# Rebuilding the head of a fused attention and feed-forward kernel

## The chip, the cores and the metric

The kernel runs on one core of a Trainium2 chip. The metric is the device time of one execution in microseconds (us). Engines are named as the profile names them: PE is TensorE (matmuls; PEld are its weight loads), DVE is VectorE, ACT is ScalarE, POOL is GpSimd, and SP issues most DMAs. A "q" behind a name (SPq, ACTq) is that engine's queue of issues.

## What is computed

2048 tokens of 512 features are normalised. A linear attention with 32 heads of 16 and a feed-forward layer of 1792 with the Mish activation both read the normalised tokens, and both are added to the input.

```
xn = _layernorm(x, axis=-1)
return x + _A_ref(xn, A_wqkv, A_w_phi, A_wo) + _B_ref(xn, B_w1, B_b1, B_w2)

# _A_ref
pq = einsum("bhsd,hdf->bhsf", q, w_phi);  pk = einsum("bhsd,hdf->bhsf", k, w_phi)
phi_q = concat([softmax(pq), softmax(-pq)], -1);  phi_k = concat([softmax(pk), softmax(-pk)], -1)
kv = einsum("bhsf,bhsd->bhfd", phi_k, v);  z = einsum("bhsf->bhf", phi_k)
o = einsum("bhqf,bhfd->bhqd", phi_q, kv) / (einsum("bhqf,bhf->bhq", phi_q, z)[..., None] + 1e-6)
return o.transpose(...) @ wo
# _B_ref
h = x @ w1 + b1;  return (h * tanh(softplus(h))) @ w2
```

## The kernel before

The tokens are 16 tiles of 128, in four groups of four (`NG`, `TPG`). The order of all instructions is written by hand: each engine runs its own instructions in the order of the program text, and waits where it needs another engine's or a DMA's result.

The head (L368 to L437) loads inputs and weights and brings group 0 up to its first projection. `fold_turn` (L87) transposes the k part of the weights on PE, 4 x 4 blocks, and ACT copies them to `wT`. `fold` (L101) multiplies them by `Wbd`, a block-diagonal form of `w_phi` (eight blocks of 16x16, made by multiplying `w_phi` with a 0/1 block mask, L409), which gives the folded weight `wkp`. The mask is made on PE (L400): `h16`, an 8x128 selection made on POOL, is multiplied by itself into `pm` in PSUM. `KVmask` (L419, L420) is a copy of it.

`ln_stats` (L118) makes mean and variance on DVE and the reciprocal root on POOL; `ln_apply` (L133) makes the normalised tile `xn` on DVE. For group 0 PE transposes `xn` (`ln_turn_pe`, L144); for the other groups a DMA does (`ln_turn_dma`, L152, issued by SP, two tiles at a time), and the result is `xnT`. `logits` (L196) projects a tile with `wkp` and ACT copies the result to `p_sb`; `value` (L168) projects it with `wv` into `vext`; `hidden` (L176) does units of the first feed-forward layer, four matmuls of 512 columns each, and ACT applies Mish with the bias `b1f`. `extremes` (L202, ten DVE operations) subtracts each head's maximum and minimum; `exponentials` (L227) follow on ACT, two instructions.

The loop over stages `s` (L441) does, for each stage: exponentials of group `s`, `accumulate` of the group before, values, the next group's logits, statistics and transposes of the group after next, `normalise`, and some hidden units, 16 in stage 0. The last loop (L469) makes the attention outputs and the second layer.

All PE results of the head and of the loop (`ptrw`, `ptr`, `pfold`, `pproj`, `ph`, `pm`) share one ring of four PSUM buffers (tag "mm", L59), taken in program order: PE can start a result only when the one four places earlier has been copied out by ACT or DVE.

In the head SP issues, in order: tiles 0-1, 2-3 and 4-7 of `x`, `w1_sb`, `wv`, the q part of `wqk`, tiles 8-15, `w2_sb`, `wo`, and then the two DMA transposes of group 1 (L153). ACT issues the k part of `wqk` and `wsrc` (`w_phi`); POOL issues the bias `b1b`, element by element across partitions.

Of the kernel before, what the change touches and what calls it, by code (L numbers as in the profile page):

```python
# [17 lines left out]
def kernel(  # L18
# [30 lines left out]
    b1_v = B_b1.rearrange("(f p) -> p f", p=P)  # L49
# [21 lines left out]
    b1b = wts.tile([P, FT], BF16, name="b1b")  # L71
# [7 lines left out]
    h16 = consts.tile([8, 8, 16], BF16, name="h16")  # L79
# [322 lines left out]
    st1 = ln_stats(2, 2)
    wT = fold_turn(D)

    nc.sync.dma_start(wo_sb, wo_v[:, :, :])
    xn = lnp.tile([P, TPG, D], BF16, name="xn", tag="xn")
    ln_apply(0, 2, *st0, xn, 0)
# [27 lines left out]
    normal(TPG, st, xn)  # L435
    extremes(0)
# [4 lines left out]
    for s in range(5):  # L441
        exponentials(s)
        if s > 0:
            accumulate(s - 1)
        if s < NG:
            for i in range(2):
                value(s * TPG + i, dve)
        for i in range(TPG):
            logits(s + 1, i, act)
        if s < NG:  # L450
            for i in range(2, TPG):
                value(s * TPG + i, act)
# [12 lines left out]
        hidden((16, 14, 6, 10, 4)[s])
        extremes(s + 1)
# [55 lines left out]
```

## Time and profile before

| | us |
|---|---|
| median of 3 runs (206.18 to 208.66) | 208.13 |
| the profiled execution | 208.03 |
| its span, first to last instruction | 206.30 |
| PE busy | 180.4 (87%) |
| DVE busy | 166.1 (81%) |
| ACT busy | 112.4 (54%) |
| POOL busy | 8.6 (4%) |

The busy shares are averages over stages with different limits: DVE is busy nearly throughout the middle of the kernel, PE throughout its last third, and neither in the head. What a change in the head is worth is read from the waits there: who waits last for whom, until one engine works on without a pause. All times below are microseconds from the span's start. In a timeline row, the bracket at the end is the engine's idle time before the row and what released it.

### The profile page before, as it was taken

Reading aid. Unit: us, or ns where it says so; the run is one execution under the profiler, and the core shown is the slowest. Engines: PE = TensorE matmul, PEld = TensorE weight load, DVE = VectorE, ACT = ScalarE, POOL = GpSimd, SP = SyncE. Lnnn points to the kernel's source line nnn. Section 1 sums busy time; section 2 is a strip of 40 time slices with the busy share of each in tenths; the row PEclk is TensorE's granted clock in tenths of the full one; section 3 lists DMA queues with packets and bytes.
Section 4 is the critical chain, followed back from the end, with each engine's and each line's share of the span. In section 5 each row is a group of like instructions: output and inputs, shape, how many; then the busy total and the mean of one; then the engine's idle time right before and its main releaser. Section 6 shows DMA issues by size and latency. Waiting matters only on the chain.

```text
span 206.3 us, 2689 instructions
## 1 busy us (share of the span) xinstructions
PE 180.4 (87%) x1026; PEld 91.8 (44%) x1041; DVE 166.1 (81%) x270; ACT 112.4 (54%) x141; POOL 8.6 (4%) x22
## 2 busy tenths in 40 slices
PE   0399729999999999899998787599999999999993
PEld 0374303445544464464454243244554455445541
DVE  2857999991599989998999999988879998954502
ACT  2348774887988789999988945131603152000000
POOL 5302001000020000000000000000000000000000
PEclk9999966999999999999999999579999999999998
DMA  5999993100005000000000560763156515567041
GB/s 147 263 385 348 348 143 65 38 0 0 3 2 102 0 3 0 0 3 0 0 0 4 97 106 2 146 126 84 54 102 130 125 51 105 104 152 101 4 102 51
DMA packets 41132, 18.02 MB, mean 87 GB/s; under 512 B 32672, under 2 KB 40608, under 8 KB 41120
## 3 DMA queue, kind: packets, MB, share of 16 engines
q1 hardware_dynamic: 40016, 17.31, 36.6%
q10 hardware_dynamic: 1056, 0.54, 1.1%
q8 instruction: 8, 0.13, 0.3%
q0 software_dynamic: 48, 0.00, 0.1%
q14 instruction: 4, 0.03, 0.1%
HBM read 7.88 MB, written 2.10 MB: 48 GB/s over the span
## 4 chain that ended last, share of the span: by engine, by line
PE 47%; DVE 36%; DMA 9%; ACT 3%; issue 2%; POOL 1%; SPq 0%
PE po L349 20%; DVE s L234 9%; PE pproj L162 8%; PE po L357 7%; PE ph L182 7%; DVE m L211 5%; DMA xnT<-xn 5%; DVE e L244 4%; DVE e L220 4%; DVE stats L124 3%; PE pnd L328 3%; ACT e L230 3%; DVE r L269 3%; DMA x_sb<-in_A_x_dram 3%; DMA ob<-ob 2%
## 5 line engine op out<-in xcount | busy, mean ns | idle before, releaser
L182 PE MATMUL ph<-xnT,w_sb 128*128 128x512 bf16 x224 | 49.3, 379 | 1.8 <-ACT p_sb L200 1.8
L349 PE MATMUL po<-w_sb,acts 128*128 128x512 bf16 x218 | 49.3, 379 | 0.3
L230 ACT ACTIVATE e<-e 128x2048 bf16<-128x2048 bf16 x16 | 29.7, 1902 | 21.9 <-DVE e L220 21.9
L189 ACT ACTIVATE acts<-ph,b1f 128x512 bf16<-128x512 f32 x56 | 36.3, 688 | 4.7 <-PE ph L182 4.6
L234 DVE TENSOR_REDUCE s<-e 128x128 f32<-128x2048 bf16 x16 | 36.4, 2276 | 1.1 <-ACT e L230 1.1
L182 PEld LDWEIGHTS <-w_sb 128*128 128x128 bf16 x224 | 21.9, 98 | 28.3 <-issue 2.1
L349 PEld LDWEIGHTS <-acts 128*128 128x128 bf16 x224 | 21.7, 98 | 25.5
L162 PEld LDWEIGHTS <-xnT 128*128 128x128 bf16 x192 | 19.3, 102 | 29.8 <-DMA xnT<-xn 5.6
L200 ACT CAST p_sb<-pproj 128x512 bf16<-128x512 f32 x32 | 17.5, 587 | 22.7 <-PE pproj L162 21.3
L162 PE MATMUL pproj<-wkp,xnT 128*128 128x512 bf16 x62 | 16.4, 417 | 5.4 <-DMA xnT<-xn 5.2
L357 PE MATMUL po<-wqk,ob 128*128 128x512 bf16 x62 | 16.4, 411 | 2.8 <-DMA ob<-ob 2.8
L364 DVE TENSOR_TENSOR x_sb<-po,x_sb 128x512 bf16<-128x512 f32 x16 | 10.6, 686 | 8.6 <-PE po L357 8.6
L162 PE MATMUL pproj<-wqk,xnT 128*128 128x512 bf16 x62 | 15.1, 392 | 0.3 <-issue 0.2
L162 PE MATMUL pproj<-wv,xnT 128*128 128x512 bf16 x61 | 15.0, 379 | 0.2
L124 DVE BATCH_NORM_STATS2 stats<-x_sb 128x6 f32<-128x512 bf16 x16 | 10.0, 680 | 3.3 <-DMA x_sb<-in_A_x_dram 3.3
L211 DVE TENSOR_TENSOR m<-m 128x512 bf16<-128x512 bf16 (+1 forms) x32 | 11.5, 358 | 1.1
L211 DVE TENSOR_TENSOR m<-p_sb 128x1024 bf16<-128x1024 bf16 x16 | 11.0, 684 | 1.1 <-ACT p_sb L200 1.1
L337 DVE TENSOR_TENSOR ob<-pnd,rd 128x512 bf16<-128x512 f32 x16 | 11.1, 692 | 0.6
L170 DVE CAST vext<-pproj 128x512 bf16<-128x512 f32 x8 | 5.4, 689 | 7.4 <-PE pproj L162 7.2
L357 PEld LDWEIGHTS <-ob 128*128 128x128 bf16 x64 | 6.4, 103 | 10.5 <-DMA ob<-ob 3.0
L336 DVE RECIPROCAL rd<-pnd 128x32 f32<-128x32 f32 x16 | 5.6, 350 | 6.6 <-PE pnd L328 6.6
L328 PE MATMUL pnd<-kvm,qT 128*128 128x136 bf16 x128 | 9.1, 223 | 2.1 <-DMA qT<-e 1.3
(52 smaller groups left out, 149.1 us busy)
## 6 DMA issues: line engine op xcount, KB each, us to landing
w_sb<-in_B_w_dram SPq DMA_DIRECT2D x2, 1792.0 KB, 14.3
out_dram<-x_sb SPq DMA_DIRECT2D x16, 128.0 KB, 1.8
x_sb<-in_A_x_dram SPq DMA_DIRECT2D x1, 1024.0 KB, 14.4
wqk<-in_A_wqkv_dram ACTq DMA_DIRECT2D x1, 512.0 KB, 5.2
x_sb<-in_A_x_dram SPq DMA_DIRECT2D x2, 256.0 KB, 4.8
x_sb<-in_A_x_dram SPq DMA_DIRECT2D x1, 512.0 KB, 8.0
wv<-in_A_wqkv_dram SPq DMA_DIRECT2D x1, 512.0 KB, 13.0
wqk<-in_A_wqkv_dram SPq DMA_DIRECT2D x1, 512.0 KB, 13.4
```

What stands on the lines that cost most here:

```text
L124: nc.vector.bn_stats(stats[:, i, :], x_sb[:, t0 + i, :])
L162: nc.tensor.matmul(pp[:], lhsT=xnT[:, t, kt, :], rhs=w[:, kt, :], start=(kt == 0), stop=(kt == KT - 1),)
L182: nc.tensor.matmul(ph[:], lhsT=w1_sb[:, kt, f * P : (f + 1) * P], rhs=xnT[:, g * TPG : (g + 1) * TPG, kt, :], start=(kt == 0), stop=(kt == ...
L189: nc.scalar.activation(acts[:, f, g * 512 : (g + 1) * 512], ph[:], ACT.Mish, bias=b1f[:, f : f + 1])
L200: copy(p_of[s][:, i, :], pp[:])
L211: nc.vector.tensor_tensor(out=m[:], in0=src[:, :, 0:half], in1=src[:, :, half : 2 * half], op=op)
L230: nc.scalar.activation(v, v, ACT.Exp)
L234: nc.vector.reduce_sum(t[:], e_of[s][:, :, 2 * k : 2 * k + 2, :].rearrange("p l t (c e) -> p l (t c) e", e=16), axis=AX.X,)
L328: nc.tensor.matmul(pnd[:, j, 0:136], lhsT=qT[:, pl * 8 + i * 4 + j, :], rhs=kvm[:, 2 * j + pl, :], start=(pl == 0), stop=(pl == 1),)
L337: nc.vector.tensor_tensor(out=o_t[:, i, :].rearrange("p (j h d) -> p j h d", j=4, d=16), in0=pnd[:, :, 0:128].rearrange("p j (h d) -> p j ...
L349: nc.tensor.matmul(po[:], lhsT=acts[:, f, t * P : (t + 1) * P], rhs=w2_sb[:, f, :], start=(f == 0), stop=False,)
L357: nc.tensor.matmul(po[:], lhsT=oT[:, i * 4 + j, :], rhs=wo_sb[:, j, :], start=False, stop=(j == 3),)
```

## The change

The block mask is made on POOL over 128 partitions (`block`, two selections) instead of by a matmul, and `KVmask` and `Wbd` read it from SBUF. ACT now issues `wsrc` first, then the k part of `wqk`, then the bias, which is loaded as 14 rows of 128 and transposed on PE into `pb`; DVE makes `b1f` from that. SP issues `wv` as its third load. Four late loads (tiles 8-15, the q part of `wqk`, `w2_sb`, `wo`) are issued behind the two DMA transposes of group 1 instead of ahead of them. On PE the fold follows the transposes of tiles 0 and 1 as before, but on DVE its casts now stand ahead of `xn` of tiles 2 and 3, and `value(0)` stands on PE between the fold and the transposes of tiles 2 and 3, cast by ACT; stage 0 makes `value(1)` alone at its start.

```diff
-    b1_v = B_b1.rearrange("(f p) -> p f", p=P)
+    b1_v = B_b1.rearrange("(f p) -> f p", p=P)
...
     nc.sync.dma_start(x_sb[:, 0:2, :], x_v[:, 0:2, :])
+    with nc.allow_non_contiguous_dma(reason="tiny w_phi load"):
+        nc.scalar.dma_start(wsrc[:], wphi_v)
+    nc.sync.dma_start(x_sb[:, 2:4, :], x_v[:, 2:4, :])
     nc.scalar.dma_start(wqk[:, :, D : 2 * D], wqkv_v[:, :, D : 2 * D])
-    nc.sync.dma_start(x_sb[:, 2:4, :], x_v[:, 2:4, :])
-    with nc.allow_non_contiguous_dma(reason="tiny w_phi and bias loads"):
-        nc.scalar.dma_start(wsrc[:], wphi_v)
-        nc.gpsimd.dma_start(b1b[:], b1_v[:, :])
+    nc.sync.dma_start(wv[:], wqkv_v[:, :, 2 * D : 3 * D])
+    nc.scalar.dma_start(b1b[:], b1_v[:, :])
     nc.sync.dma_start(x_sb[:, 4:8, :], x_v[:, 4:8, :])
     nc.sync.dma_start(w1_sb[:], w1_v[:, :, :])
-    nc.sync.dma_start(wv[:], wqkv_v[:, :, 2 * D : 3 * D])
-    nc.sync.dma_start(wqk[:, :, 0:D], wqkv_v[:, :, 0:D])
-    nc.sync.dma_start(x_sb[:, 8:16, :], x_v[:, 8:16, :])
-    nc.sync.dma_start(w2_sb[:], w2_v[:, :, :])
...
-    nc.gpsimd.memset(h16[:], 1.0)
-    nc.gpsimd.affine_select(
-        out=h16[:], in_=h16[:], pattern=[[1, 8], [0, 16]], compare_op=ALU.is_equal,
-        fill=0.0, base=0, channel_multiplier=-1,
-    )
+    nc.gpsimd.memset(block[:], 1.0)
+    for sign in (1, -1):
+        nc.gpsimd.affine_select(
+            out=block[:], in_=block[:], pattern=[[-16 * sign, 8], [0, 16]],
+            compare_op=ALU.is_ge, fill=0.0, base=0 if sign == 1 else 15,
+            channel_multiplier=sign,
+        )
...
-    pm = ps.tile([P, 512], FP32, name="pm", tag="mm")
-    h16f = h16[:].rearrange("p h d -> p (h d)")
-    nc.tensor.matmul(pm[:, 0:P], lhsT=h16f, rhs=h16f, start=True, stop=True)
...
     for i in range(2):
         ln_turn_pe(i, xn, i, act)
+    fold(wT, wkp, (0, 1))
     ln_apply(2, 2, *st1, xn, 2)
-    fold(wT, wkp, (2, 3))
+    value(0, act)
     for i in range(2, 4):
         ln_turn_pe(i, xn, i, dve)
-    nc.vector.tensor_copy(b1f[:], b1b[:])
+    pb = ps.tile([P, 512], BF16, name="pb", tag="mm")
+    nc.tensor.transpose(pb[:, 0:FT], b1b[:], ident[0:FT, 0:FT])
     for i in range(TPG):
         logits(0, i, act)
+    nc.vector.tensor_copy(b1f[:], pb[:, 0:FT])
...
     normal(TPG, st, xn)
+    nc.sync.dma_start(x_sb[:, 8:16, :], x_v[:, 8:16, :])
+    nc.sync.dma_start(wqk[:, :, 0:D], wqkv_v[:, :, 0:D])
+    nc.sync.dma_start(w2_sb[:], w2_v[:, :, :])
+    nc.sync.dma_start(wo_sb, wo_v[:, :, :])
...
-            for i in range(2):
+            for i in range(0 if s else 1, 2):
                 value(s * TPG + i, dve)
```

The order of SP's queue at the start of the program, before (-) and after (+); `w_sb` stands for `w1_sb` (128x4x1792) and `w2_sb` (128x14x512), and a row of `wqk` from `in_A_wo_dram` is the load of `wo`:

```order
-L378 DMA x_sb<-in_A_x_dram 128x8x512
-L379 DMA w_sb<-in_B_w_dram 128x14x512
-L405 DMA wqk<-in_A_wo_dram 128x4x512
-L153 DMA_TRANSPOSE xnT<-xn 128x8x128 x6
...
+L376 DMA w_sb<-in_B_w_dram 128x4x1792
+L153 DMA_TRANSPOSE xnT<-xn 128x8x128 x2
+L431 DMA x_sb<-in_A_x_dram 128x8x512
+L432 DMA wqk<-in_A_wqkv_dram 128x4x512
+L433 DMA w_sb<-in_B_w_dram 128x14x512
+L434 DMA wqk<-in_A_wo_dram 128x4x512
+L153 DMA_TRANSPOSE xnT<-xn 128x8x128 x4
```

Two of the six transposes moved ahead of four loads; ahead of them stand `wv` and what was there before.

The order on DVE between the first statistics (L124) and those of tiles 4 to 7, before and after:

```order
+L401 TENSOR_TENSOR Wbd<-block,wsrc 128x512
+L135 TENSOR_SCALAR xn<-x_sb,mv,rstd 128x512 x2
 L124 BN_STATS stats<-x_sb 128x6 x2
 L126 BN_AGGR mv<-stats 128x2 x2
+L114 CAST wkp<-pfold 128x512 x2
 L135 TENSOR_SCALAR xn<-x_sb,mv,rstd 128x512 x2
-L409 TENSOR_TENSOR Wbd<-pm,wsrc 128x512
-L135 TENSOR_SCALAR xn<-x_sb,mv,rstd 128x512 x2
-L419 COPY KVmask<-pm 128x128
-L420 COPY KVmask<-pm 128x8
-L114 CAST wkp<-pfold 128x512 x2
 L150 COPY xnT<-ptr 128x512 x2
```

`Wbd` and `xn` of tiles 0 and 1 moved ahead of the statistics of tiles 2 and 3, the casts of the fold ahead of `xn` of those, and the two `KVmask` copies to the start of the program.

## Rows read from the trace of the kernel before

**Rows 1.** Chain of waits in order of time: start us, us, what.
```profile
1.31 5.56 DMA x_sb<-in_A_x_dram
...
15.05 2.37 DVE stats L124 x4
...
19.94 9.67 DMA xnT<-xn
```

**Rows 2.** Timeline of the head: start us, us, engine line op out<-in xcount [idle before].
```profile
4.78 1.29 DVE L124 BATCH_NORM_STATS2 stats<-x_sb 128x6 f32<-128x512 bf16 x2 [2.71 <-DMA x_sb<-in_A_x_dram]
...
5.99 1.89 PE L93 MATMUL ptrw<-ident,wqk 128*128 128x128 bf16 x16 [1.90 <-DMA wqk<-in_A_wqkv_dram]
...
6.63 2.05 ACT L98 COPY wT<-ptrw 128x512 bf16<-128x512 bf16 x4 [3.46 <-PE ptrw L93]
6.69 0.72 POOL L130 TENSOR_TENSOR rstd<-rstd,mhalf 128x2 f32<-128x2 f32 x1
...
8.94 0.68 DVE L409 TENSOR_TENSOR Wbd<-pm,wsrc 128x512 bf16<-128x512 f32 x1
9.63 0.74 DVE L135 TENSOR_SCALAR xn<-x_sb,mv,rstd 128x512 bf16<-128x512 bf16 x2
...
10.69 1.01 PE L147 MATMUL ptr<-ident,xn 128*128 128x128 bf16 x8 [2.81 <-DVE KVmask L420]
...
11.49 1.91 PE L106 MATMUL pfold<-Wbd,wT 128*128 128x128 bf16 x16
...
13.02 1.29 DVE L114 CAST wkp<-pfold 128x512 bf16<-128x512 f32 x2 [2.38 <-PE pfold L106]
...
14.22 0.75 DVE L150 COPY xnT<-ptr 128x512 bf16<-128x512 bf16 x2
```

**Rows 3.** Timeline from the first exponentials to stage 1.
```profile
26.53 3.71 ACT L230 ACTIVATE e<-e 128x2048 bf16<-128x2048 bf16 x2 [1.73 <-DVE e L220]
...
29.66 1.46 PE L162 MATMUL pproj<-wkp,xnT 128*128 128x512 bf16 x3 [5.15 <-DMA xnT<-xn]
...
31.64 0.59 ACT L200 CAST p_sb<-pproj 128x512 bf16<-128x512 f32 x1 [1.39 <-remote]
...
37.06 13.98 PE L182 MATMUL ph<-xnT,w_sb 128*128 128x512 bf16 x64
...
53.83 0.69 DVE L170 CAST vext<-pproj 128x512 bf16<-128x512 f32 x1 [6.71 <-PE pproj L162]
```

**Rows 4.** Stretches: us; busy of PE, PEld, DVE, ACT, POOL; granted clock; DMA share; GB/s.
```profile
28.00:30.00 2.00, 0.34 (x1) 0.13 (x2) 2.00 (x5) 2.00 (x2) 0.00 (x0) 0.50 0.89 198
...
34.00:36.00 2.00, 2.00 (x11) 0.85 (x10) 1.93 (x4) 1.05 (x2) 0.00 (x0) 0.95 0.80 153
...
130.00:131.00 1.00, 0.00 (x0) 0.00 (x0) 0.93 (x3) 0.00 (x0) 0.00 (x0) 0.50 0.89 174
```

**Rows 5.** Timeline of PE: two later waits.
```profile
114.46 3.61 PE L182 MATMUL ph<-xnT,w_sb 128*128 128x512 bf16 x16 [1.83 <-ACT p_sb L200]
...
131.34 3.59 PE L357 MATMUL po<-wqk,ob 128*128 128x512 bf16 x8 [2.77 <-DMA ob<-ob]
```

**Rows 6.** DMA issues: out<-in engine op xcount, KB each, median us to landing.
```profile
x_sb<-in_A_x_dram SPq DMA_DIRECT2D x1, 1024.0 KB, 14.4
...
xnT<-xn SPq DMA_TRANSPOSE x6, 3.2
...
wsrc<-in_A_w_phi_dram ACTq DMA_DIRECT2D x1, 16.0 KB, 5.8
```

**Rows 7.** GB/s in 40 slices; queues, 4.5 to 5.0 (q10 ACT's, q1 SP's); one stretch.
```profile
GB/s 147 263 385 348 348 143 65 38 0 0 3 2 102 0 3 0 0 3 0 0 0 4 97 106 2 146 126 84 54 102 130 125 51 105 104 152 101 4 102 51
...
q10 hardware_dynamic: 188, 0.19, 107.6%
q1 hardware_dynamic: 1, 0.00, 0.6%
...
7.50:8.00 0.50, 0.38 (x4) 0.11 (x2) 0.50 (x2) 0.50 (x2) 0.00 (x0) 1.00 1.33 102
```

More of the change, by code (lines that the diff above doesn't have):

```diff
@@ L70 @@
     w2_sb = wts.tile([P, FT, D], BF16, name="w2_sb")
-    b1b = wts.tile([P, FT], BF16, name="b1b")
+    b1b = wts.tile([FT, P], BF16, name="b1b")
     b1f = wts.tile([P, FT], FP32, name="b1f")
@@ L78 @@
     mhalf = consts.tile([P, TPG], FP32, name="mhalf")
-    h16 = consts.tile([8, 8, 16], BF16, name="h16")
+    block = consts.tile([P, 8, 16], BF16, name="block")
     KVmask = consts.tile([P, 136], FP32, name="KVmask")
@@ L393 @@
         nc.vector.memset(pkv[b][:, :, 0:136], 0.0)
+    nc.vector.tensor_copy(KVmask[:, 0:P], block[:].rearrange("p h d -> p (h d)"))
+    nc.vector.tensor_copy(KVmask[:, P : P + 8], block[:, :, 0])
     dve, act = nc.vector.tensor_copy, nc.scalar.copy
-    pm = ps.tile([P, 512], FP32, name="pm", tag="mm")
-    h16f = h16[:].rearrange("p h d -> p (h d)")
-    nc.tensor.matmul(pm[:, 0:P], lhsT=h16f, rhs=h16f, start=True, stop=True)
+    wT = fold_turn(D)
     st0 = ln_stats(0, 2)
[L402 to L407, printed above, removed]
     nc.vector.tensor_tensor(
         out=Wbd[:].rearrange("p j (h e) -> p j h e", h=8),
-        in0=pm[:, 0:P].rearrange("p (o h e) -> p o h e", o=1, h=8).to_broadcast([P, 4, 8, 16]),
+        in0=block[:, None, :, :].to_broadcast([P, 4, 8, 16]),
         in1=wsrc[:, :, None, :].to_broadcast([P, 4, 8, 16]),
@@ L414 @@
     )
+    xn = lnp.tile([P, TPG, D], BF16, name="xn", tag="xn")
+    ln_apply(0, 2, *st0, xn, 0)
+    st1 = ln_stats(2, 2)
     for i in range(2):
         ln_turn_pe(i, xn, i, act)
+    fold(wT, wkp, (0, 1))
     ln_apply(2, 2, *st1, xn, 2)
-    nc.vector.tensor_copy(KVmask[:, 0:P], pm[:, 0:P])
-    nc.vector.tensor_copy(KVmask[:, P : P + 8], pm[:, 0:P:16])
-    fold(wT, wkp, (2, 3))
+    value(0, act)
     for i in range(2, 4):
         ln_turn_pe(i, xn, i, dve)
-    nc.vector.tensor_copy(b1f[:], b1b[:])
+    pb = ps.tile([P, 512], BF16, name="pb", tag="mm")
+    nc.tensor.transpose(pb[:, 0:FT], b1b[:], ident[0:FT, 0:FT])
     for i in range(TPG):
         logits(0, i, act)
+    nc.vector.tensor_copy(b1f[:], pb[:, 0:FT])
     def normal(t0, st, xn):
```

## The prediction

> **What bounds the kernel now.** I read the chain of waits first, then the timeline of the stretches that it names, then the granted clock, then the DMA issues and queues.
>
> The chain of waits [rows 1] runs on VectorE (DVE) through the statistics of token tiles 4 to 7, then through the DMA transpose of their normalised values, 9.67 us from 19.94. Behind it PE works without a pause into stage 1, and DVE is the bound of the middle of the kernel. So two things hold the head: DVE's work up to that transpose, and the transpose itself. DVE stood idle for 6.71 us before the cast at 53.83 [rows 3], waiting for `value(4)` of PE. That is how much PE can come earlier before DVE binds; from there on every stage follows and the gain is carried to the end.
>
> The span is 206.30 us and the execution 208.03 us, 1.73 us around it. The median of three runs is 208.13, so I count against 208.03.
>
> **What the transpose really holds.** Its wait idles PE for 5.15 us, to 29.66 [rows 3]. But look at ACT in the same rows: the exponentials of stage 0 run from 26.53 for 3.71 us, and only then does ACT cast `logits(1)` out of PSUM (31.64). PE has four PSUM buffers in this ring, so even with xnT at hand it would fill them and stop until ACT has cast the first. With the exponentials where they are, the best case is: exponentials end 30.24, cast 0.59, then `value(2)` and `value(3)` at 4 x 0.216 us each (64 matmuls in 13.98 us is 0.218), and `hidden(16)` begins at 32.6 instead of 37.06: 4.45 us. More comes only from an earlier end of the first `extremes`, that is from DVE's head.
>
> **The new head on DVE and PE.** The key arrival is the k part of `wqk`. It landed at 5.99, when L93 starts [rows 2]; `wsrc`, the last of the four first loads, at 1.30 + 5.8 = 7.1 [rows 6]. After the change `wsrc` goes ahead on ACT's queue and the load of tiles 2 and 3 is issued at about the same moment as `wqk`. The four together are the same bytes, so `wqk` lands between 5.99 and 7.1: I take the middle, 6.5.
> - PE: 16 transposes 1.89, to 8.4. ACT's last copy of `wT` comes 2.69 after their start (6.63 + 2.05 - 5.99), 9.2.
> - DVE meanwhile: tile 0 lands at 4.78, statistics 1.29, aggregates, GpSimd's power (0.72, ends 7.41), and `xn` of two tiles 0.74 to 8.15. `Wbd` (0.68) now sits between, while DVE waits for GpSimd. The two PE transposes of tokens go 8.4 to 9.4 (1.01); before, they waited until 10.69 for a buffer that the mask matmul held.
> - Fold: 1.91 from 9.4, the first quarter out at 10.1. DVE's two casts 1.29, 11.4; `xn` of tiles 2 and 3, 0.74, 12.1.
> - PE: fold to 11.3, `value(0)` 4 x 0.216 to 12.2, eight transposes. DVE's copies 0.75, and `b1f` behind one more small transpose 0.1: 13.45.
>
> Before, DVE reached this point at 14.96 (0.75 from 14.22) and the statistics in [rows 1] follow. So the head gains 1.5 us. Bounds: transposes and fold ran at 0.118 us each for 128 columns in the head, half the rate of `hidden(16)` (0.218 for 512); if PE is still slow at `value(0)` and the transposes, 1.1 us is lost (0.4 left); if the full rate comes during the fold, 0.6 more (2.1).
>
> **The stretch 18 to 32 us.** All is 1.5 us earlier: the transpose is issued at 18.4. The loads ahead of it are now 3.9 MB instead of 7.9 MB by the shapes in the code. At 348 GB/s [rows 7] from about 2.5, with 1.5 us for a slow stretch (below), they are through by about 15.5, so it should land in 3.2 us, the median of the six [rows 6], at 21.6. PE, through with its transposes at 12.7, has `logits(0)` and `hidden(6)` ahead, 40 matmuls at 0.216, to 21.4. So `value(1)` and three tiles of `logits(1)` fill the four buffers by 24.9. `extremes` ends at 25.0, DVE's cast 0.69 frees one buffer, the fourth tile runs to 26.6. ACT: exponentials 25.0 to 28.75, cast to 29.35; then `value(2)`, `value(3)`, and `hidden(16)` at 31.1 instead of 37.06: 5.95 us.
>
> **The clock.** PE stands still from 26.6 to 29.4, 2.8 us. The granted clock of before fell to 0.50 (1.2 of 2.4 GHz) in the wait that began at 24.5, and rose again at about 34.2 [rows 4]; PE worked from 29.66 in it, so 4.54 / 2 = 2.27 us were lost. It fell a second time around a wait of 2.77 us, and not after one of 1.83 [rows 4, 5]. My gap is as long as the one that cost the clock, and a shorter idle stretch (24.9 to 25.7) lies ahead of it, so I expect the fall, and price it as before: 2.3 us. Bounds: nothing, or 3.1, half of the 6.2 us from 28 to 34.2, if PE works in all of such a stretch.
>
> **What costs nothing, and its cover.** Two mask selections of 128x128 on GpSimd replace one of 8x128, but the bias DMA that GpSimd issued (1.3 us) is gone; the mask is done before tile 0 lands at 4.78, and so are DVE's two mask copies. ACT issues one more DMA (0.5 us) before its table load, done by 4, needed at 7. `value(0)` is only moved. `wv` has 1.6 MB with it and is needed at 11.3; tiles 4 to 7 at 13.5; `w1` at 16. The late loads, 3.9 MB from about 21, are through by some 33 at 348 GB/s [rows 7]; the transposes of stage 0 queue behind them, land by 37, and are read at about 50. Tiles 8 to 15 are read first at 25.7 by the statistics and should land at about 26 (an estimate: 3.0 us for 1.05 MB at 348 GB/s, and 2 us for its start). DVE has slack there: it reaches the wait for `value(4)` 1.5 + 0.69 us earlier, at 44.9, and PE delivers at 50.1, so 5.2 us. If that cover were gone, each later microsecond would count.
>
> **Sum.** 208.03 - 4.45 - 1.5 + 2.27 = 204.35; I say 204.3. Its own range is 203.0 to 205.8.
>
> **A rule against this.** Between 4.5 and 5.0 us ACT's queue sent 188 packets and SP's queue one, though SP's second load was issued at 1.31: the first loads were served one after another [rows 1, 7]. The Trainium skill, in "DMA: Bandwidth & Descriptors", Queues, rings and completion order, says that each DMA engine takes packets in turn from the queues with work. That row does not agree. By the rule `wqk` would share its time with the load of tiles 2 and 3 and then with `wv`, as in the second rival.
>
> **Rivals.**
> 1. *The clock stays up* (0.24). For it: a wait of 1.83 us did no harm [rows 5]. Against: 2.77 us did. 208.03 - 5.95 = 202.1.
> 2. *`wqk` comes late* (0.19). It shares its time with 0.5 MB that SP has queued: 0.52 MB at 385 GB/s [rows 7] is 1.36 us after 5.99, 7.4, 0.9 later than I count, 205.2. Also, the rate fell to 102 GB/s at 7.5 to 8 [rows 7], behind the 32-byte runs of `wsrc` and the 2-byte pieces of the bias; two microseconds at such a rate instead of 385 lose 1.5. If `wsrc` was the cause, the loss now falls on the loads that PE waits for: up to 206.7. The Trainium skill, in the same page's Specifications, asks for at least 512 B a piece and says that smaller ones are read, modified and written; the slow stretch (102 GB/s) agrees, but either load could have made it.
> 3. *The transposes stay slow* (0.06): 9.67 us whatever is ahead. They land at 28.1, `logits(1)`, `value(2)`, `value(3)` take 5.2 us from there, `hidden(16)` at 33.3, with the clock down: 206.5 to 207.
> 4. *Tiles 8 to 15 land late, and it is slower* (0.04). Their load is issued at about 21 instead of 5.96. If it took 14.4 us as before [rows 6], it would land at 35.4, 9.7 after DVE wants it; less the slack of 5.2, 4.5 come back: 208.8. It decides from a landing after 34.6. Against it: before, some 3 MB were queued ahead; now only the transposes are.
>
> **How the numbers follow.** My forecast has 0.47. The range 201.5 to 206.9 leaves out the fast end of rival 1, the slow ends of 2 and 3, and 4, about 0.15. Faster than 2% (about what can be told from no change) means under 204.0: most of rival 1 and two fifths of the forecast, 0.43. Slower by over 2% needs rival 4 and more on top: 0.03. The rest, 0.54, is within.
>
> **What would show it.** Right: L93 starts at about 6.5; the statistics of tiles 4 to 7 at about 13.4; the transpose lands about 3.2 us after its issue; PE's first matmul after the exponentials at about 29.4 behind a wait for ACT and not for a DMA; `hidden(16)` at about 31 plus what the clock takes; granted clock 0.50 for some microseconds from 28; DVE's wait for `value(4)` still there, near 5 us. Wrong: DVE waiting for `x_sb` after 26, L93 after 7.5, or no wait left before `value(4)`.

## The result and the profile after

The changed kernel takes 200.21 us (median of 4 runs, 199.6 to 200.6) against 208.3 (4 runs, 206.18 to 208.66): a ratio of 0.963, with a 95% interval of 0.956 to 0.970. Here and below a median counts all runs of a kernel, and a ratio only those within 1.5% of its fastest. The forecast was 204.3 with a range of 201.5 to 206.9; the gain is about 8 us where 3.8 was forecast. The profiled execution took 200.60 us with a span of 198.9, so 1.7 lie around it as before, and the working below counts 208.03 against 200.60.

Rows of the timeline after: start us, us, engine line op out<-in xcount, and in the bracket the idle time before and its releaser.

```profile
6.31 1.89 PE L93 MATMUL ptrw<-ident,wqk 128*128 128x128 bf16 x16 [6.31 <-DMA wqk<-in_A_wqkv_dram]
...
8.84 1.62 PE L106 MATMUL pfold<-Wbd,wT 128*128 128x128 bf16 x16
...
10.30 1.03 PE L162 MATMUL pproj<-wv,xnT 128*128 128x512 bf16 x4
...
12.36 2.46 DVE L124 BATCH_NORM_STATS2 stats<-x_sb 128x6 f32<-128x512 bf16 x4
...
17.34 2.67 SPq L153 DMA_TRANSPOSE xnT<-xn  x2
...
20.06 1.20 SPq L431 DMA_DIRECT2D x_sb<-in_A_x_dram  x1
...
21.97 3.63 PE L162 MATMUL pproj<-wkp,xnT 128*128 128x512 bf16 x16 [0.31 <-DMA xnT<-xn]
...
27.62 2.47 DVE L124 BATCH_NORM_STATS2 stats<-x_sb 128x6 f32<-128x512 bf16 x4 [3.12 <-DMA x_sb<-in_A_x_dram]
28.17 1.89 PE L162 MATMUL pproj<-wv,xnT 128*128 128x512 bf16 x8 [2.57 <-ACT p_sb L200]
29.89 13.98 PE L182 MATMUL ph<-xnT,w_sb 128*128 128x512 bf16 x64
...
47.06 1.28 DVE L170 CAST vext<-pproj 128x512 bf16<-128x512 f32 x2
```

Read it beside [rows 2, 3]. The statistics of tiles 4 to 7 start at 12.36 (14.96 before, 2.60 earlier). PE's wait of 5.15 us for `xnT` has shrunk to 0.31; what is left of the hole is 2.57 us, and ACT ends it. `hidden(16)` starts at 29.89 instead of 37.06, 7.17 earlier. And DVE, which waited 6.71 us for `value(4)`, now casts it at 47.06 with no bracket at all: DVE arrives last. Its own wait is new and lies further up: 3.12 us for tiles 8 to 15.

The chain of waits of after, in order of time, goes through that load:

```profile
1.30 4.96 DMA wqk<-in_A_wqkv_dram
...
20.06 7.54 DMA x_sb<-in_A_x_dram
27.62 2.47 DVE stats L124 x4
```

The granted clock, in stretches of 2 us (columns as in [rows 4]):

```profile
26.00:28.00 2.00, 0.00 (x0) 0.00 (x0) 0.38 (x1) 2.00 (x2) 0.00 (x0) 1.00 1.03 352
28.00:30.00 2.00, 1.83 (x9) 0.87 (x9) 2.00 (x4) 2.00 (x5) 0.00 (x0) 1.00 1.08 365
...
124.00:126.00 2.00, 2.00 (x6) 0.76 (x5) 1.92 (x5) 0.00 (x0) 0.00 (x0) 0.50 0.44 83
```

PE stands still from 26 to 28 and the clock stays at 1.00 (2.4 GHz). It falls to 0.50 (1.2 GHz) only once, later, around the wait for `ob`:

```profile
123.68 3.60 PE L357 MATMUL po<-wqk,ob 128*128 128x512 bf16 x8 [2.15 <-DMA ob<-ob]
```

**Two sums that describe every run below.** From the profiled execution of each kernel I read where `hidden(16)` starts (H), where the statistics of tiles 8 to 11 start (S), and where DVE casts `value(4)` (V). Before, V - H = 16.77. In after, V - S = 47.06 - 27.62 = 19.44, with DVE working on its own chain (19.43 fits the other rows). So V is the later of H + 16.77 and S + 19.43, and the rest of the kernel follows V. In the table, "rest" is span less V; "clock" is the mean granted clock of the profiled execution.

| kernel | L93 | stats 4-7 | H | S | V | rest | clock | profiled, us | median, us |
|---|---|---|---|---|---|---|---|---|---|
| before | 5.99 | 14.96 | 37.06 | 27.62 | 53.83 | 152.5 | 0.963 | 208.03 | 208.30 |
| after | 6.31 | 12.36 | 29.89 | 27.62 | 47.06 | 151.8 | 0.980 | 200.60 | 200.21 |
| after, again (a2) | 7.23 | 14.26 | 33.43 | 29.02 | 50.22 | 149.3 | 0.991 | 201.22 | 199.87 |
| e1 late loads | 5.81 | 14.81 | 32.35 | 30.50 | 49.93 | 151.2 | 0.992 | 202.78 | 202.68 |
| e2 e1 and mask | 5.79 | 12.88 | 30.41 | 26.87 | 47.18 | 151.7 | 0.991 | 200.56 | 201.37 |
| e3 head only | 6.61 | 13.29 | 35.00 | 25.35 | 51.77 | 152.1 | 0.964 | 205.60 | 205.17 |
| e4 tiles 8-15 early | 7.36 | 14.35 | 33.51 | 26.40 | 50.28 | 149.3 | 0.991 | 201.28 | 200.86 |
| e5 value(0) back | 6.26 | 12.32 | 29.85 | 28.40 | 47.84 | 149.0 | 1.000 | 198.54 | 200.01 |
| e6 bias by elements | 6.48 | 13.26 | 32.33 | 29.03 | 49.10 | 151.6 | 0.980 | 202.42 | 201.81 |
| e8 longer gap | 7.60 | 13.66 | 32.87 | 28.00 | 50.83 | 150.8 | 0.983 | 203.33 | 203.30 |
| e10 bias by rows alone | 5.81 | 14.78 | 35.01 | 27.43 | 51.78 | 152.5 | 0.972 | 206.02 | 205.47 |
| b1 early, two casts | 6.28 | 12.27 | 28.08 | 25.52 | 44.95 | 150.7 | 0.991 | 197.45 | 197.63 |
| b2 two casts | 6.24 | 13.31 | 29.13 | 28.55 | 47.99 | 150.7 | 0.991 | 200.38 | 199.99 |
| b3 b1, `wqk` first | 5.70 | 12.89 | 28.70 | 26.14 | 45.56 | 149.2 | 1.000 | 196.48 | 196.64 |

The rule gives V to within 0.1 us in every row but e8, whose clock is still low during the first part of `hidden(16)` (15.16 us for its 64 matmuls instead of 13.98). The rest is 149.0 to 149.3 where the clock holds to the end, and 150.7 to 152.5 where it falls once at the wait for `ob`.

One more thing is needed to read the times: the kernel before does not have one time. Over all the runs taken beside the experiments it took 204.3 to 204.9 us at a mean granted clock of 0.992, 205.7 to 206.5 at 0.98 (0.980 to 0.983), and 207.7 to 208.8 at 0.964. The profiled execution has 0.963: two slow stretches, from 27.4 to 34.2 and from 129.8 to 136.6 (6.8 us each, from 1 us windows of the clock). After the change most runs have 0.98 to 0.99. At 0.989 to 0.991 they took 199.5 to 201.2 and at 1.0 198.6. So at one clock, near 0.99, the change is worth some 4.6 us (204.6 to about 200); the remaining 3 or so of the 8 are slow stretches of the clock that the kernel before usually has and the changed one usually has not. This split is an estimate: the mean clock does not say where in an execution it was low.

### The profile page after: what moved, and what is told of

Read it like the earlier page. It is cut to its first block, busy times and chain, and to the rows that moved or that the text cites. A ratio compares the mean times of both kernels' runs of the same rounds, so it can differ in the third digit from the quotient of the medians.

```text
span 198.9 us, 2704 instructions
## 1 busy us (share of the span) xinstructions
PE 179.1 (90%) x1041; PEld 90.7 (46%) x1041; DVE 165.4 (83%) x269; ACT 112.4 (56%) x142; POOL 7.6 (4%) x22
## 4 chain that ended last, share of the span: by engine, by line
PE 55%; DVE 29%; DMA 8%; ACT 4%; issue 2%; POOL 1%; ACTq 0%; SPq 0%
PE po L349 21%; PE pproj L162 10%; PE ph L182 9%; PE po L357 8%; DVE s L234 7%; DVE m L211 5%; DMA x_sb<-in_A_x_dram 4%; DVE e L244 3%; DVE e L220 3%; PE pnd L328 3%; ACT e L230 3%; DMA wqk<-in_A_wqkv_dram 2%; DVE stats L124 2%; PE pkv L295 2%; DVE r L269 2%
## 5 line engine op out<-in xcount | busy, mean ns | idle before, releaser
L162 PEld LDWEIGHTS <-xnT 128*128 128x128 bf16 x192 | 18.8, 99 | 26.5 <-issue 5.7
L162 PE MATMUL pproj<-wqk,xnT 128*128 128x512 bf16 x64 | 15.7, 402 | 0.0
L162 PE MATMUL pproj<-wkp,xnT 128*128 128x512 bf16 x64 | 14.5, 379 | 0.3 <-DMA xnT<-xn 0.3
L124 DVE BATCH_NORM_STATS2 stats<-x_sb 128x6 f32<-128x512 bf16 x16 | 10.0, 681 | 4.3 <-DMA x_sb<-in_A_x_dram 4.3
L244 DVE TENSOR_TENSOR e<-e,r 128x1024 bf16<-128x1024 bf16 x16 | 10.4, 689 | 0.3
```

Of the source, the lines that this page charges most:

```text
L124: nc.vector.bn_stats(stats[:, i, :], x_sb[:, t0 + i, :])
L162: nc.tensor.matmul(pp[:], lhsT=xnT[:, t, kt, :], rhs=w[:, kt, :], start=(kt == 0), stop=(kt == KT - 1),)
L244: nc.vector.tensor_tensor(out=v, in0=v, in1=r2[:, :, None, :].to_broadcast([P, 64, 8, 2]), op=ALU.mult)
```

## The experiments

**e1: the late loads alone.** The kernel before, with the four late loads behind group 1's transposes.

```diff
-    nc.sync.dma_start(wqk[:, :, 0:D], wqkv_v[:, :, 0:D])
-    nc.sync.dma_start(x_sb[:, 8:16, :], x_v[:, 8:16, :])
-    nc.sync.dma_start(w2_sb[:], w2_v[:, :, :])
...
-    nc.sync.dma_start(wo_sb, wo_v[:, :, :])
...
     normal(TPG, st, xn)
+    nc.sync.dma_start(x_sb[:, 8:16, :], x_v[:, 8:16, :])
+    nc.sync.dma_start(wqk[:, :, 0:D], wqkv_v[:, :, 0:D])
+    nc.sync.dma_start(w2_sb[:], w2_v[:, :, :])
+    nc.sync.dma_start(wo_sb, wo_v[:, :, :])
```

> The kernel before with one change: tiles 8-15, the q part of wqk, w2 and wo are issued behind the two DMA transposes of group 1. Theory (PSUM ring): PE's 5.15 us wait goes, but PE stops instead until ACT has cast the first tile of logits(1) behind the exponentials; hidden(16) at about 32.6 (37.06 before), a gain of 4.4 at most. The statistics of tiles 8-15 then wait for their load (7.5 us from its issue in the changed kernel, so to about 30), which takes some 0.2 back: about 204 us if the clock stays up in the gap, about 206 if it falls. Rival (the stall and the slow clock all come back, 5.15 + 2.27): about 200.9, and then the rebuilt head would be worth next to nothing.

202.68 us (202.43 to 202.86), ratio 0.984 (0.977 to 0.991). From its timeline:

```profile
10.54 1.01 PE L147 MATMUL ptr<-ident,xn 128*128 128x128 bf16 x8 [2.84 <-DVE KVmask L416]
...
14.81 2.47 DVE L124 BATCH_NORM_STATS2 stats<-x_sb 128x6 f32<-128x512 bf16 x4
...
24.84 1.90 PE L162 MATMUL pproj<-wkp,xnT 128*128 128x512 bf16 x7 [0.22 <-DMA xnT<-xn]
...
30.50 2.47 DVE L124 BATCH_NORM_STATS2 stats<-x_sb 128x6 f32<-128x512 bf16 x4 [2.94 <-DMA x_sb<-in_A_x_dram]
30.62 1.89 PE L162 MATMUL pproj<-wv,xnT 128*128 128x512 bf16 x8 [1.72 <-ACT p_sb L200]
32.35 13.98 PE L182 MATMUL ph<-xnT,w_sb 128*128 128x512 bf16 x64
```

This is the prediction's first term by itself: `hidden(16)` at 32.6 was worked out, 32.35 was measured, and the wait that remains is for ACT's first cast behind the exponentials, as the ring of four buffers demands. The gap is 1.72 us and the clock stays up in it. Not foreseen in the prediction, and put at 0.2 us in the expectation above: DVE already waits for tiles 8 to 15 (S + 19.43 = 49.93 = V), so 0.8 us of what PE won is not used. The time is still 1.3 us below the 204 that was expected with the clock up, as much as the rest of the kernel is shorter than before (151.2 for 152.5).

**e2: the mask on GpSimd, added to e1.** `block` in place of the matmul, with the two `KVmask` copies at the start of the program, and nothing else of the head.

```diff
-    pm = ps.tile([P, 512], FP32, name="pm", tag="mm")
-    h16f = h16[:].rearrange("p h d -> p (h d)")
-    nc.tensor.matmul(pm[:, 0:P], lhsT=h16f, rhs=h16f, start=True, stop=True)
...
-        in0=pm[:, 0:P].rearrange("p (o h e) -> p o h e", o=1, h=8).to_broadcast([P, 4, 8, 16]),
+        in0=block[:, None, :, :].to_broadcast([P, 4, 8, 16]),
```

> As e1_late_loads, and the block mask is made on GpSimd, so that KVmask is copied early and the mask holds no PSUM buffer. Theory: the first PE transposes of tokens start when xn is ready (about 9 instead of 10.69), the statistics of tiles 4-7 at about 13.6 instead of 14.96, and all behind it moves by as much: about 1.3 us less than e1_late_loads, some 202.7. Rival (the order of the first loads and the fold's place make the head faster, not the mask): the same time as e1_late_loads.

201.37 us (200.46 to 202.27), ratio 0.979 (0.969 to 0.989). From its timeline:

```profile
8.58 1.03 PE L147 MATMUL ptr<-ident,xn 128*128 128x128 bf16 x8 [0.91 <-DVE xn L135]
...
12.88 2.46 DVE L124 BATCH_NORM_STATS2 stats<-x_sb 128x6 f32<-128x512 bf16 x4
...
28.68 1.89 PE L162 MATMUL pproj<-wv,xnT 128*128 128x512 bf16 x8 [1.72 <-ACT p_sb L200]
30.41 13.98 PE L182 MATMUL ph<-xnT,w_sb 128*128 128x512 bf16 x64
```

With the k part of `wqk` at the same moment (5.79 and 5.81), the statistics of tiles 4 to 7 start 1.93 us earlier than in e1, and `hidden(16)` 1.94. So the mask is most of what the head gains in H (1.94 of the 2.46 us between e1 and after): PE's wait ahead of the token transposes, 2.84 us until the mask had been copied out of its buffer, is 0.91 us, until `xn` is ready. In the medians it is about half (1.3 of 2.5 us).

**e3: the head without the late loads.** The changed kernel with the four late loads where they were before.

```diff
     nc.sync.dma_start(w1_sb[:], w1_v[:, :, :])
+    nc.sync.dma_start(wqk[:, :, 0:D], wqkv_v[:, :, 0:D])
+    nc.sync.dma_start(x_sb[:, 8:16, :], x_v[:, 8:16, :])
+    nc.sync.dma_start(w2_sb[:], w2_v[:, :, :])
...
+    nc.sync.dma_start(wo_sb, wo_v[:, :, :])
...
-    nc.sync.dma_start(x_sb[:, 8:16, :], x_v[:, 8:16, :])
-    nc.sync.dma_start(wqk[:, :, 0:D], wqkv_v[:, :, 0:D])
-    nc.sync.dma_start(w2_sb[:], w2_v[:, :, :])
-    nc.sync.dma_start(wo_sb, wo_v[:, :, :])
```

> The changed kernel with the four late loads back ahead of the transposes of group 1. Theory: the head is 2.6 us earlier on DVE, but the transposes land behind all loads, at about 28 instead of 29.6 (the slow stretch of the bias load is gone), PE stands still for about 6 us, the clock falls, and hidden(16) starts at about 35.5: 206.5 us. So head and late loads are worth little apart (1.7 and 4.3) and more together. Rival (the parts add up): 8.1 less what e1_late_loads gains, about 204.

205.17 us (201.94 to 205.6, 10 runs), ratio 0.982 (0.975 to 0.989).

```profile
27.59 3.17 PE L162 MATMUL pproj<-wkp,xnT 128*128 128x512 bf16 x7 [4.98 <-DMA xnT<-xn]
...
35.00 13.98 PE L182 MATMUL ph<-xnT,w_sb 128*128 128x512 bf16 x64
...
51.77 0.69 DVE L170 CAST vext<-pproj 128x512 bf16<-128x512 f32 x1 [6.92 <-PE pproj L162]
```

The statistics are 1.67 us earlier than before. PE still waits 4.98 us for a transpose that needs 9.3 us from its issue, but that lands at 27.59 instead of 29.66, and `hidden(16)` is 2.06 earlier. The time lies between the theory's 206.5 and the rival's 204, but as the rival has it, the parts nearly add up. In the medians late loads alone gain 5.0 us (207.68 to 202.68), the head alone 2.5 (to 205.17), and both 7.9 to 8.1. In V it is 3.90 and 2.06, and 6.77 for both. At a clock near 0.99 it is about 2.1 (202.4 to 202.9 for 204.3 to 204.9) and 2.6 (201.9 and 202.2), and 4.6 for both. So at most 0.8 us comes from having the two parts together.

**a2: the changed kernel again,** unchanged, in another set of runs.

> The changed kernel once more, for more executions beside those of the next kernels. Theory (whether the clock falls in the 2.6 us gap of PE at 25.6 is open in each execution): times spread over about 199.5 to 202, higher where the mean granted clock is lower. Rival (the gap never costs the clock): all within 199.6 to 200.6 as the first four.

199.87 us (198.57 to 201.22, 6 runs). Its profiled execution is the slowest of the six, and it is worth most of all the runs:

```profile
7.23 1.89 PE L93 MATMUL ptrw<-ident,wqk 128*128 128x128 bf16 x16 [7.23 <-DMA wqk<-in_A_wqkv_dram]
...
11.47 1.78 PE L162 MATMUL pproj<-wv,xnT 128*128 128x512 bf16 x4
...
30.06 3.55 PE L162 MATMUL pproj<-wv,xnT 128*128 128x512 bf16 x8 [2.55 <-ACT p_sb L200]
33.43 14.00 PE L182 MATMUL ph<-xnT,w_sb 128*128 128x512 bf16 x64
```

and the granted clock (columns as in [rows 4]):

```profile
30.00:32.00 2.00, 1.94 (x5) 0.69 (x5) 2.00 (x8) 1.51 (x5) 0.14 (x1) 0.51 1.09 361
32.00:34.00 2.00, 2.00 (x7) 0.76 (x6) 2.00 (x2) 0.90 (x2) 1.12 (x2) 0.63 1.10 348
```

The same program as in the rows of after. But `wqk` landed 0.92 later, `value(0)` took 1.78 us for 1.03 (the granted clock reads 1.00 there in both, so the records do not show why), and behind a gap as long as there (2.55 and 2.57) the clock fell, so that the eight matmuls of `value(2)` and `value(3)` took 3.55 instead of 1.89. `hidden(16)` starts at 33.43; the forecast, with its fall of the clock, was 31.1 + 2.27 = 33.4. And yet the time is 201.2 and not 204.3, because in this execution the clock holds at the wait for `ob`: the rest is 149.3 and not 152.5.

**e4: tiles 8 to 15 early.** Their load right behind that of `w1`; the other late loads stay late.

```diff
     nc.sync.dma_start(w1_sb[:], w1_v[:, :, :])
+    nc.sync.dma_start(x_sb[:, 8:16, :], x_v[:, 8:16, :])
...
-    nc.sync.dma_start(x_sb[:, 8:16, :], x_v[:, 8:16, :])
```

> The changed kernel with the load of tiles 8-15 issued right behind w1, in the stretch in which no DMA runs (13.5 to 18.5), and the other three late loads left where they are. Theory: DVE's 3.12 us wait for these tiles at 27.6 goes, DVE is ready at about 44, and PE's value(4), at 46.65 instead of DVE's 47.06, sets the pace: 0.4 us less than the changed kernel, 199.8; the transposes still land about 3.2 us after their issue. Rival (the load delays the transposes or w1): the same or slower, 200.2 to 201.

200.86 us (197.87 to 201.28, 6 runs), ratio 0.968 (0.957 to 0.979). From its timeline:

```profile
26.40 2.46 DVE L124 BATCH_NORM_STATS2 stats<-x_sb 128x6 f32<-128x512 bf16 x4
...
30.15 3.53 PE L162 MATMUL pproj<-wv,xnT 128*128 128x512 bf16 x8 [2.59 <-ACT p_sb L200]
...
50.28 0.69 DVE L170 CAST vext<-pproj 128x512 bf16<-128x512 f32 x1 [4.38 <-PE pproj L162]
```

The expected 199.8 was missed by 1.1 us, and not for the rival's reason. DVE's wait is gone (S = 26.40, no bracket), but in the profiled execution `wqk` is late (7.36), PE has its gap of 2.59 us, loses 1.64 us to the clock behind it, and binds (V = H + 16.77 = 50.28). Only the one run at clock 1.0 can be set against one of the changed kernel at that clock, 197.87 against 198.57. With DVE's bound moved, PE's stands next to it.

**e5: `value(0)` back in stage 0.** It is cast by DVE again and leaves the head.

```diff
-    value(0, act)
...
-            for i in range(0 if s else 1, 2):
+            for i in range(2):
```

> The changed kernel with value(0) back at the start of stage 0, cast by DVE there. Theory: PE idles in the head for the same time instead, and the cast of 0.65 us on DVE falls into its wait for tiles 8-15: no change, 200.2 within 0.5. Rival (value(0) in the head gives back its 0.86 us of PE, or brings the clock up earlier): 0.9 us slower.

200.01 us (198.54 to 201.1), no difference from 199.87 and 200.21. The value tile of the head costs and brings nothing that can be told here. PE's gap is 1.73 us instead of 2.6, since `value(0)` now lies behind the transposes, but DVE has one cast more and binds by tiles 8 to 15 (28.40 + 19.43 = 47.83, V = 47.84).

**e6: the bias by elements again.** The changed kernel with the bias loaded by GpSimd across partitions, and without its transpose.

```diff
-    nc.scalar.dma_start(b1b[:], b1_v[:, :])
+    with nc.allow_non_contiguous_dma(reason="tiny bias load"):
+        nc.gpsimd.dma_start(b1b[:], b1_v[:, :])
...
-    pb = ps.tile([P, 512], BF16, name="pb", tag="mm")
-    nc.tensor.transpose(pb[:, 0:FT], b1b[:], ident[0:FT, 0:FT])
```

> The changed kernel with the bias loaded element by element across partitions on GpSimd, as before the change, and without its transpose on TensorE. Theory: the slow stretch of DMA between 6.5 and 9 us, which the kernel before had (102 GB/s at 7.5 to 8.0) and the changed kernel has not, comes back, and the loads of tiles 4-7 and w1 land later by 1 to 2 us; the head's chain on TensorE hangs on none of them before 12.4, so the time moves by 0 to 0.8: 199.9 to 201. Rival: the stretch came from wsrc, which is made of short runs too and now comes first; then no slow stretch, and 200.2.

201.81 us (200.95 to 202.56, 4 runs), ratio 0.977 (0.968 to 0.986): 0.8 us above the expected range. The stretch 7 to 8 us, first of after, then of e6:

```profile
7.00:8.00 1.00, 1.00 (x13) 1.00 (x11) 1.00 (x4) 1.00 (x3) 0.00 (x0) 1.00 1.09 346
```

```profile
7.00:8.00 1.00, 1.00 (x12) 1.00 (x11) 0.82 (x3) 0.87 (x2) 0.14 (x1) 1.00 0.75 101
```

and the queues of e6 from 6.5 to 8.5 us (packets, MB, time as a share of 16 engines):

```profile
q1 hardware_dynamic: 280, 0.27, 65.7%
q0 software_dynamic: 48, 0.00, 40.6%
```

Forty-eight packets of GpSimd's queue, 3.5 KB in all, take 41% of all sixteen engines for two microseconds. `wsrc`, with its 32-byte runs, is loaded in both kernels, so it is the bias that makes the slow stretch. The forecast could not tell the two apart, and weighed `wsrc` in its second rival. Whether the 2-byte pieces or GpSimd's queue make the bias so dear is open: the edit changes both. The Trainium skill, "DMA: Bandwidth & Descriptors", Specifications, asks for at least 512 B a transfer for the full rate. The trace agrees for the bias (101 GB/s); while 437 packets of ACT's queue, most of `wsrc` in runs of 32 B, pass in after from 3.0 to 3.5 us, the rate is 281 GB/s.

**e10: the bias by rows alone,** in the kernel before.

```diff
-        nc.gpsimd.dma_start(b1b[:], b1_v[:, :])
+    nc.scalar.dma_start(b1b[:], b1_v[:, :])
...
+    pb = ps.tile([P, 512], BF16, name="pb", tag="mm")
+    nc.tensor.transpose(pb[:, 0:FT], b1b[:], ident[0:FT, 0:FT])
```

> The kernel before, with one part of the change alone: the bias loaded as 14 rows by ScalarE and transposed on TensorE, instead of element by element on GpSimd. Theory: the bias made the slow stretch of DMA at 7 to 9 us (119 GB/s at 7 to 8), and its being on GpSimd's queue makes each transpose of ob land half a microsecond later (3.2 against 2.7 us from its issue). Then the rate at 7 to 8 us is above 300 GB/s; the loads ahead of group 1's transposes are through 1 to 1.5 us earlier, so xnT lands near 28.3 instead of 29.6, hidden(16) starts near 36 instead of 37.06, the wait for ob is 2.15 instead of 2.77, and the time is 1 to 2 us below the kernel before: 205.5 to 207. Rival: wsrc made the stretch, or the landing of ob hangs on something else of the change; then 207.5 to 208 with a wait of 2.77.

205.47 us (201.43 to 207.56, 10 runs), ratio 0.983 (0.974 to 0.991). The rate at 7 to 8 us is 388 GB/s (119 before), and `xnT` lands at 28.13 instead of 29.66:

```profile
28.13 5.31 PE L162 MATMUL pproj<-wkp,xnT 128*128 128x512 bf16 x15 [2.88 <-DMA xnT<-xn]
```

At equal clock it is about 1.2 us faster than before (203.28 against 204.34 at 0.992, one run each; 207.2 and 207.6 against 208.5 to 208.8 at 0.964). The other half of the theory fell: the wait for `ob` stays at 2.75.

**e8: a longer gap.** The changed kernel with two more copies on ACT between the exponentials of stage 0 and the casts; they go to a tile that nothing reads.

```diff
+        if s == 0:
+            for _ in range(2):
+                nc.scalar.copy(pad[:], xn[:, 0, :])
```

> The changed kernel with two copies of 128x512 on ACT, into a tile that nothing reads, between the exponentials of stage 0 and the casts of logits(1): PE's gap grows from 2.6 to about 3.6 us. If the clock does not care: PE 1.0 later, of which 0.4 is slack against DVE, so 200.8. Theory (a longer gap costs the clock in most executions): the granted clock falls at about 28 for 3.4 to 6.8 us and the time is 202 to 203.5.

203.3 us (198.99 to 204.1, 6 runs). The gap is 3.76 us in the profile, and the clock falls behind it, at 31.8, when PE has worked for 1.2 us:

```profile
30.64 2.43 PE L163 MATMUL pproj<-wv,xnT 128*128 128x512 bf16 x8 [3.76 <-ACT p_sb L201]
32.87 15.16 PE L183 MATMUL ph<-xnT,w_sb 128*128 128x512 bf16 x64
```

A microsecond of gap costs 3.3 in the median, most of it through the clock: five of the six runs have a mean clock of 0.972 to 0.983 and take 202.1 to 204.1; the sixth, at 1.0, takes 198.99, next to the 198.57 of the kernel without the copies.

**b1: both bounds at once.** Tiles 8 to 15 early, as in e4, and two of group 1's four logits tiles cast by DVE, so that PE's buffers come free during the exponentials.

```diff
-            logits(s + 1, i, act)
+            logits(s + 1, i, dve if s == 0 and i < 2 else act)
```

> A version meant to be faster: the load of tiles 8-15 right behind w1 as in e4_x8_early, and the first two tiles of logits(1) cast by DVE instead of ACT, so that PE gets two buffers back before the exponentials end. Theory: PE's gap shrinks from 2.6 to about 0.9 us, hidden(16) starts at 28.2, DVE's chain (two casts more, no wait for the load) and PE both reach value(4) at about 45.3 instead of 47.06, and the clock never falls there: 198.4, and little spread. Rival (DVE is the bound and pays for the casts): about 200.

197.63 us (196.55 to 200.3, 6 runs), ratio 0.954 (0.949 to 0.960): faster than both kernels, and 0.8 us faster than expected, though its runs spread over nearly 4 us where little was expected.

```profile
24.33 1.28 DVE L200 CAST p_sb<-pproj 128x512 bf16<-128x512 f32 x2
...
25.52 2.46 DVE L124 BATCH_NORM_STATS2 stats<-x_sb 128x6 f32<-128x512 bf16 x4
28.08 13.98 PE L182 MATMUL ph<-xnT,w_sb 128*128 128x512 bf16 x64 [0.86 <-ACT p_sb L200]
...
44.95 1.45 DVE L170 CAST vext<-pproj 128x512 bf16<-128x512 f32 x2
```

The gap is 0.86 us, the clock stays up in the head, and both engines reach `value(4)` within 0.1 us of each other (28.08 + 16.77 = 44.85; 25.52 + 19.43 = 44.95).

**b2: the two casts without the early load.**

> The changed kernel, with the first two of group 1's logits tiles cast by VectorE instead of ScalarE; the load of tiles 8-15 stays behind the transposes. It takes the two changes of the fastest version so far apart. Theory (two bounds that have to be moved together): the gap of TensorE ahead of value(4) shrinks from 2.6 to about 0.9 us and hidden(16) starts near 28.1, but VectorE still waits for tiles 8-15 until about 27.6 and reaches value(4) near 47, against 44.95 with both changes. So 199.0 to 199.6 at a mean clock of 0.99, some 1.7 above the version with both, and no fall of the clock in the head. Rival: the load is not the bound, the gap is all; then it equals the version with both, 197.6.

199.99 us (198.06 to 200.41, 6 runs), ratio 0.967 (0.961 to 0.974).

```profile
28.55 2.48 DVE L124 BATCH_NORM_STATS2 stats<-x_sb 128x6 f32<-128x512 bf16 x4 [1.89 <-DMA x_sb<-in_A_x_dram]
29.13 13.98 PE L182 MATMUL ph<-xnT,w_sb 128*128 128x512 bf16 x64 [0.75 <-ACT p_sb L200]
```

PE is early, DVE waits for the load, and V is 47.99, by S; the time is 0.4 us above the expected range and rules out the rival's 197.6. In the medians neither edit alone gains on the changed kernel's 199.87 to 200.21 (early load 200.86, casts 199.99), and both together are at 197.63. At clock 1.0 the four kernels are at 198.57 (changed), 197.87 (early load), 198.06 (casts), and 196.55 to 197.23 (both): 0.7 and 0.5 by themselves, 1.3 to 2.0 together, from one or two runs of each.

**b3: b1 with the k part of `wqk` ahead of `wsrc`** on ACT's queue, as before the change.

```diff
-    with nc.allow_non_contiguous_dma(reason="tiny w_phi load"):
-        nc.scalar.dma_start(wsrc[:], wphi_v)
...
     nc.scalar.dma_start(wqk[:, :, D : 2 * D], wqkv_v[:, :, D : 2 * D])
+    with nc.allow_non_contiguous_dma(reason="tiny w_phi load"):
+        nc.scalar.dma_start(wsrc[:], wphi_v)
```

> The fastest version so far (tiles 8-15 loaded early, two casts by VectorE), with ScalarE issuing the k part of wqk ahead of wsrc again, as before the change. Theory: the k part lands at 5.8 to 6.0 in every execution (with wsrc ahead it landed between 6.3 and 7.6, a few packets behind wv's), so the head's chain begins up to 1.3 us earlier when it would have been late; wsrc lands later, near 6.5, and delays Wbd on VectorE, whose statistics of tiles 0-3 end near 5.3. Expected median 197.0 to 197.6 with less spread. Rival: Wbd, waiting for wsrc, holds up xn of tiles 0-1 and with it the transposes on TensorE by more than the earlier k part gives back; then 198 to 198.5.

196.64 us (196.25 to 197.58, 6 runs), ratio 0.954 (0.949 to 0.960). L93 starts at 5.70, but the statistics of tiles 4 to 7 start at 12.89, later than in b1 (12.27): the early start is lost again before them. At clock 1.0 the two kernels overlap (196.25 to 196.72, and 196.55 to 197.23). What differs is that four of b3's six runs hold that clock, and two of b1's. Whether the order of the two loads does that is open.

## Why the prediction was wrong, point by point

The bookkeeping from the forecast to the profiled execution: 204.35; less 2.27, as the clock did not fall in the head; less 1.21, as `hidden(16)` started at 29.89 and not at 31.1; plus 0.40, as DVE and not PE decided V (47.06 for 29.89 + 16.77 = 46.66); less 0.66, as the rest (with the time around the span) is that much shorter, 151.8 and not 152.5. That is 200.61, and 200.60 was measured.

- **The transpose and the ring: right.** The term of 4.45 us stands. e1 shows it alone (32.35 for 32.6), and after shows PE waiting for ACT behind the exponentials and not for the DMA. The transposes of group 1 landed 4.6 us after the first was issued and not 3.2, which cost PE 0.31.
- **The head: right in order, too small in size.** 1.5 us forecast, 2.60 measured. `wqk` landed at 6.31, 0.2 earlier than assumed. From there to the statistics of tiles 4 to 7 the forecast counted 6.95 us, and after took 6.05. That is 0.9 less, past the 0.6 that the text named for a full rate already in the fold. From the start of the fold to the start of `value(0)` it was 1.46 us where 1.9 was counted; another 0.4 lies ahead of the fold, where the sum adds the busy times of rows of which each begins some 0.2 before the one ahead of it has ended. The 6.05 is not certain either: a2, b2 and e4 needed 7.0 to 7.1. That they match the sum is luck: `value(0)`, at 1.7 to 1.8, took 0.7 us more there than was counted, and the steps ahead of it 0.6 less.
- **`wqk` late (second rival): it happens, at times.** It landed between 6.2 and 7.6 wherever ACT issues `wsrc` first and SP `wv` third, and between 5.7 and 6.0 with `wqk` first. From 4.0 to 5.0 us in after, ACT's queue sent 309 packets and SP's 34, much as in [rows 7]; from 5.0 to 7.5 it was 228 and 697, and both were served. The Trainium skill, "DMA: Bandwidth & Descriptors", Queues, rings and completion order, says that engines take packets in turn from the queues with work. The traces lie between that rule, by which the forecast put `wqk` at 7.4, and the row: three of the nine such kernels have it at 7.2 to 7.6, six at 6.2 to 6.6. What decides between the two is open.
- **The clock: the step that failed.** "I expect the fall, and price it as before: 2.3 us." In the profiled execution of after the term came to nothing: the clock stayed at 1.00. The gap was forecast well (2.8; 2.57 measured), but whether it costs the clock changes from run to run of the same program, and the sum counted it in full. Over the profiled executions, PE's gap in the head came with a fall, inside it or up to 1.2 us behind its end, in all with 2.88 us or more (before, e3, e8, e10), in none with 1.73 or less (e1, e2, e5, b1 to b3), and in three of four between 2.55 and 2.59 (a2, e4, e6, but not after; where it fell, 1.5 to 1.7 us were lost, and not 2.3). At the wait for `ob` it fell in all five executions with 2.7 to 2.8 us, and in five of nine with 2.15. So the length of the gap alone does not settle it, and the cause stays open.
- **The remainder was taken as fixed: a second step that failed.** The sum starts from one execution that had two slow stretches, and carries the second, in the rest of 152.5 us, through unexamined. Without it the rest is 149.0 to 149.3. That stretch lies at the wait for `ob`, which is 2.77 us before and 2.15 after; why it is shorter is open (last section). a2 shows this: it meets the forecast for `hidden(16)` to 0.1 us and is still 3 us faster than the forecast, all of it in the rest. So the chance of a quick result was far above the 0.24 of the first rival: two stretches could stay out, not one, and that rival still ended at 202.1.
- **The cover of tiles 8 to 15: wrong, and cheap.** They landed 7.5 us after the issue and not 5. The slack of 5.2 was reckoned against a PE that delivers `value(4)` at 50.1, after a loss to the clock. With PE at 46.66, and DVE there at 43.94 were it not for its wait, the slack is 2.7, and the wait of 3.12 uses it up: DVE arrives at `value(4)` at 47.06, as early as before the change (53.83 - 6.71 = 47.12). Two of the signs that the forecast named for being wrong are there: DVE waits for `x_sb` after 26, and no wait is left before `value(4)`. All that the head gave DVE, it lost again at that load. The fourth rival had the place right and the size wrong: 0.4 us, not 4.5, since the load needed 7.5 us and not 14.4.
- **The bias: a part without a term.** Its load was named only as one of two possible causes of the slow stretch. The forecast kept 1.5 us for that stretch in the landing of the loads, as if it stayed. e10 gives the edit's worth alone, about 1.2 us at equal clock, and e6 what the changed kernel would lose without it, 1.6 to 1.9 in the median. Part of the latter is the clock: at 0.98 it is 201.2 to 202.6 against 200.5 and 200.6.

## What to carry to other kernels

A forecast made from one execution inherits its accidents: look for stretches of low clock in it, ask for each whether the change can move or end it, and put both outcomes in the range, those far from the edit too. Slack is only as good as the engine it is reckoned against; when the forecast speeds that engine up, reckon it again, here by the later of two sums (PE's and DVE's) for the same instruction. Where two engines arrive within a microsecond of each other, an edit that moves one of them shows almost nothing, and both must be moved together.

## What was not expected of the hardware

- The same program, behind gaps of 2.55 and 2.57 us of PE, kept its clock in one execution and lost it in another, for 1.66 us (3.55 for eight matmuls that take 1.89). The slow stretches here last 6.8 us (before, twice; the end of after) or 3.4 (a2 from 30.05 to 33.46).
- 3.5 KB of bias in pieces of 2 bytes, on GpSimd's queue, held the rate of all DMA engines at 101 to 119 GB/s from 7 to 8 us (e6, before), where it is 346 to 388 with the bias by rows (after, e10).
- The DMA transposes of `ob` land 3.2 us after their issue (median of eight) in before, e1, e2 and e6, and 3.3 in e10, but 2.7 in the other nine rows of the table, 100 us after anything that was edited; the first is waited for, 2.7 to 2.8 us against 2.15. The kernels with 2.7 have both the new mask and the bias by rows. e2 and e6 lack the second and e10 the first, and each has the longer time. Why is open.
